# Sparse attention and a spectral mix on one core: channel weights read once, fewer constants, and a tail by pairs

## The chip, the cores and the metric

The kernel runs on one core of a Trainium2 chip. A core has TensorE (PE, matrix multiplication into PSUM), VectorE (DVE), ScalarE (ACT), GpSimd (POOL) and SyncE (SP), and 16 transfer engines (DMA) that move data between HBM and the on-chip memory. The metric is the device time of one execution in microseconds (us), the median of several runs.

## The reference, cut to what matters

Attention with two kinds of masks, then a spectral mixing layer over the result. B = 8, S = 576, 8 heads of 64, so D = 512, and 64 Fourier modes.

```python
# heads 0 to 3: local mask (0 <= i - j < 32); heads 4 to 7: strided (j <= i and i = j mod 32)
attn = softmax(where(mask, q @ k.T / 8, -1e9)); x = (attn @ v) as (8, 576, 512)

X = np.fft.rfft(x, axis=1)[:, :64]                    # real part Xr, imaginary part Xi
Yr = einsum('bmd,mde->bme', Xr, w_r) - einsum('bmd,mde->bme', Xi, w_i)
Yi = einsum('bmd,mde->bme', Xr, w_i) + einsum('bmd,mde->bme', Xi, w_r)
y = np.fft.irfft(Yr + 1j * Yi (zero above mode 63), n=576, axis=1)
u = x + y
out = u + np.maximum(u @ w_ch, 0.0)
```

w_r and w_i are 64 x 512 x 512 in fp32, 67 MB each: nearly all that the kernel reads. For mode 0 the imaginary part of X is zero, and the imaginary part of Y does not count.

## The kernel before

It works in fp16 on chip; transfers issued by GpSimd convert from fp32. There are three stages. First the strided heads of the 8 batches; the weights of the first 18 modes are fetched beside them. Then the local heads, with 8 modes per batch of the first half of the 512 input rows (slot 0) beside each. Then the same 64 modes over the other half (slot 1), with `turn` and `premix` beside them: x is transposed and multiplied with the channel weights ahead of time (v0 = x @ w_ch, xo = x). Last the tail, which adds the spectral part.

Constants and weight fetches:

```python
    # cM6: 128 x 432, cM5: 128 x 360 (a mask four times over), cMa: 128 x 480, cMb: 128 x 512, fp16
    ...
    pw = ctx.enter_context(tc.tile_pool(name="pw", bufs=NWBUF))        # 12 weight buffers of 512 KB
    ...
    GUEST = {3: ("Y0", 0), 4: ("Y0", 1), 5: ("X0", 0), 6: ("X0", 1)}   # weights that sit in
    GUEST |= {16: ("YT", 0), 17: ("YT", 1)}                            # space not yet used
    ...
            for ri, src in enumerate([moe_w_r, moe_w_i]):
                nc.gpsimd.dma_start(
                    wt[ds(64 * ri, 64)],
                    src[m, ds(256 * half, 256), :].rearrange("(p c) e -> p c e", c=4),
                )
    ...
    def w_cp_fetch():      # the channel weights, rows reordered to match the transposed x
        w_cp = pw.tile([128, 4, DM], F16, tag="w", name="w_cp")
        ...                # four transfers of 128 KB
```

One mode: 16 matmuls, then the fetch of a later weight tile; after eight modes the sum is taken out of PSUM.

```python
    def mode(slot, m):
        ...
        if slot or m not in GUEST:
            w_fetch()
        if mi == 7:
            ...
            if slot == 0:
                nc.scalar.activation(out=YS["Y0"][part], in_=src, func=ACTF.Copy)
            else:
                nc.vector.tensor_tensor(
                    out=YS["YT"][part], in0=src, in1=YS["Y0"][part], op=AluOp.add
                )
```

The local stage, 19 items of attention work per batch spread over 8 modes:

```python
        for mi in range(8):
            upto = -(-len(work) * (mi + 1) // 8)
            for w in work[n:upto]:
                w()
            n = upto
            mode(0, 8 * b + mi)
    ...
    w_chs["n"] = ptr.tile([128, 4, DM], F16, name="w_ch")       # the channel weights again,
    nc.gpsimd.dma_start(w_chs["n"], moe_w_ch.rearrange("(c p) e -> p c e", p=128))   # rows in order
```

The tail. A unit (b, t) is a tile of 128 rows of the output of batch b (t = 4: the last 64 rows of two batches). Spectra of the last 16 modes are first transposed (`tp`) and multiplied with the channel weights (`zp`), and copied per batch to yys and zzs.

```python
    psum_pools(z=2, v=3, u=3)
    ...
    def unit_v0(i):
        ...
        nc.tensor.matmul(vps[i], idn, v0, start=True, stop=(t == 4))     # L803

    def unit_v(i):
        ...
        rows_v(b, t, vp)                                                 # L634: += inverse DFT of zz
        ...
        nc.scalar.activation(out=rl, in_=vp, func=ACTF.Relu)             # L812
        if pool_adds(b, t):
            nc.gpsimd.tensor_tensor(out=rl, in0=rl, in1=xo, op=AluOp.add)    # L815

    def pool_adds(b, t):
        return t in (1, 3, 4) and (b, t) != (B - 1, 3)

    def unit_u(i):
        ...
        rows_u(b, t, up, add=not pool_adds(b, t))                        # identity of xo, then yy
        ...
        nc.vector.tensor_tensor(                                         # L827
            out=osb[:, t % 2, :], in0=up, in1=rls[b, t][:, t % 2, :], op=AluOp.add
        )
        ...                                                              # stores by SyncE

    for i in range(3):
        unit_v0(i)
    spec_last(0)
    spec_out(3, 0, *held[0])
    LAG = 2
    for i in range(len(units) + LAG):
        ...          # unit_v0(i), unit_v(i), the spectra of the next batch, unit_u(i - LAG)
```

Of the kernel before, what the change touches and what calls it, by code (L numbers as in the profile page):

```python
# [15 lines left out]
B = 8  # L16
# [13 lines left out]
def _host_consts():  # L30
    s = np.arange(S)
    m = np.arange(NM)
    ang = 2.0 * np.pi * np.outer(s, m) / S
    F3 = np.stack([np.sin(ang), np.cos(ang), -np.sin(ang)], axis=1)
    F3 = F3.reshape(S, 3 * NM)

    Fl = np.zeros((128, 5, 3 * NM))
    for t in range(5):
        Fl[: SCS[t], t] = F3[128 * t : 128 * t + SCS[t]]
    Fs = np.zeros((128, 6, 3 * NM))  # L40
    for rp in range(2):
        for j, (a, z) in enumerate(JG):
            r2 = np.arange(a, z)
            ss = (32 * np.arange(NCB)[None, :] + 2 * r2[:, None] + rp).reshape(-1)
            Fs[: len(ss), 3 * rp + j] = F3[ss]

    A = np.zeros((4, 2, 16, S))
    for mm in range(NM):  # L50
        e = np.zeros(S // 2 + 1, dtype=np.complex128)
        for ri, unit in enumerate((1.0, 1j)):
            e[mm] = unit
            A[mm // 16, ri, mm % 16] = np.fft.irfft(e, n=S)
    A = A.reshape(2 * NM, S)
    A[:, :512] = A[:, :512].reshape(128, 256, 2).transpose(0, 2, 1).reshape(128, 512)

    ms = []
    for nr in (6, 5):
        n = nr * NCB  # L60
        kc, kr = np.arange(n) // nr, np.arange(n) % nr
        qr, qc = np.arange(n) // NCB, np.arange(n) % NCB
        ok = (kr[:, None] == qr[None, :]) & (kc[:, None] <= qc[None, :])
        blk = np.zeros((128, n))
        blk[:n] = np.where(ok, 0.0, NEG)
        ms.append(np.tile(blk, (1, 4)))

    rel = np.arange(160)[None, :] - np.arange(128)[:, None]
    blk = np.where((rel >= 0) & (rel < STRIDE), 0.0, NEG)
    ma = np.tile(blk, (1, 3))  # L70
    last = np.full((128, 96), NEG)
    last[:64, 32:] = blk[:64, :64]
    mb = np.tile(np.concatenate([blk, last], axis=1), (1, 2))
    f16 = [a.astype(np.float16) for a in (Fl, Fs, A, ms[0], ms[1], ma, mb)]
    return f16 + [np.eye(128, dtype=np.float16)]
# [3 lines left out]
def kernel(  # L79
# [20 lines left out]
    def psum_pools(**bufs):  # L100
        pctx.close()
        pss.clear()
        for n, c in bufs.items():
# [9 lines left out]
    hosts = _host_consts()  # L113
    names = ["cFl", "cFs", "cA", "cM6", "cM5", "cMa", "cMb", "cI"]
    drams = {
# [10 lines left out]

    idn = cs["cI"]


# [34 lines left out]
    def w_fetch(n=1):  # L164
        for _ in range(n):
# [9 lines left out]
            else:  # L175
                wt = pw.tile([128, 4, DM], F16, tag="w", name="wt")
            for ri, src in enumerate([moe_w_r, moe_w_i]):
                nc.gpsimd.dma_start(  # L178
# [4 lines left out]

    def w_cp_fetch():
        w_cp = pw.tile([128, 4, DM], F16, tag="w", name="w_cp")
        for c2 in range(2):
            for half in range(2):
                nc.gpsimd.dma_start(
                    w_cp[ds(64 * c2, 64), ds(2 * half, 2), :],
                    moe_w_ch[ds(256 * half, 256), :].rearrange(  # L190
                        "(p cp c2) e -> c2 p cp e", cp=2, c2=2
                    )[c2],
                )
        w_chs["cp"] = w_cp

# [115 lines left out]
    def str_scores(b, t):  # L311
# [3 lines left out]
        n = (z - a) * NCB  # L315
        mask = cs["cM6"] if j == 0 else cs["cM5"]
        scp = psum("sc")
        nc.tensor.matmul(scp[:, 0 : 4 * n], idn, mask, start=True, stop=False)
        for h in range(4):
# [84 lines left out]
    def loc_scores(b, h, tail):  # L404
        par, hp = b % 2, h // 2
        scp = psum("sc")
        nc.tensor.matmul(  # L407
            scp if tail else scp[:, 0:480],
            idn,
            cs["cMb"] if tail else cs["cMa"],  # L410
            start=True,
# [90 lines left out]
    def mode(slot, m):  # L502
# [5 lines left out]
        yv = yp.rearrange("p (m e x) -> p m e x", m=8, e=4)  # L508
        wt = w_tiles[slot * NM + m]
        for e in range(4):  # L510
            for c in range(4):
                nc.tensor.matmul(  # L512
                    yv[:, mi, e, :],
                    wt[:, XC[c], ds(128 * e, 128)],
                    Xh[half][:, c, :, :, m],
                    start=(c == 0),
                    stop=(c == 3),
                )
        if slot or m not in GUEST:
            w_fetch()  # L520
        if mi == 7:
            part = (slice(None), slice(None), mg // 2, slice(None), ds(8 * (mg % 2), 8))
            src = yp.rearrange("p (m e x) -> p e x m", m=8, e=4)
            if slot == 0:
# [120 lines left out]

    def rows_u(b, t, up, add):
        cols = out_cols(t)
        if add:
            xo = xos[b][:, t, :] if t < 4 else xoh[b // 2]
            nc.tensor.matmul(up, idn, xo, start=True, stop=(t == 4))  # L650
        if t < 4:
            nc.tensor.matmul(up, cs["cA"][:, cols], yys[b], start=not add, stop=True)  # L652
            return
        for i in range(2):
# [3 lines left out]
                yys[b - 1 + i],  # L658
                start=not add,
                stop=True,  # L660
# [7 lines left out]
    load(1)  # L668
    const_load(nc.sync, "cMa", "cMb", "cFl", "cA")
    load(2)  # L670
# [57 lines left out]

    psum_pools(tp=2, sc=2, av=2, y=2)
    for b in range(B):  # L730
# [10 lines left out]
        if b == 6:  # L741
            work.insert(0, w_cp_fetch)
        n = 0
        for mi in range(8):
            upto = -(-len(work) * (mi + 1) // 8)
            for w in work[n:upto]:
                w()
            n = upto
            mode(0, 8 * b + mi)
    actx.close()  # L750
# [7 lines left out]
    yys = [ptr.tile([128, DM], F16, name=f"yy{i}") for i in range(B)]  # L758
    w_chs["n"] = ptr.tile([128, 4, DM], F16, name="w_ch")
    nc.gpsimd.dma_start(w_chs["n"], moe_w_ch.rearrange("(c p) e -> p c e", p=128))  # L760
    work = []
    for b in range(B):
# [11 lines left out]
    n = 0  # L774
    for m in range(NM):
        mode(1, m)
# [7 lines left out]

    psum_pools(z=2, v=3, u=3)
    units = []
    for b in range(B):
        units += [(b, 0), (b, 1)]
        if b % 2:
            units.append((b, 4))  # L790
        units += [(b, 2), (b, 3)]
    held, vps, rls, osbs = {}, {}, {}, {}
    LAST = len(units) - 1

    def spec_last(bq):
        held[bq] = psum("z", half=True), psum("z")
        spec_mm(3, bq, *held[bq])

    def unit_v0(i):
        b, t = units[i]  # L800
        vps[i] = psum("v")
        v0 = v0s[b][:, t, :] if t < 4 else v0h[b // 2]
        nc.tensor.matmul(vps[i], idn, v0, start=True, stop=(t == 4))  # L803

    def unit_v(i):
        b, t = units[i]
        vp = vps.pop(i)
        rows_v(b, t, vp)
        if t % 2 == 0:
            rls[b, t] = rls[b, t + 1] = pw.tile([128, 2, DM], FP, tag="w", name="rl")  # L810
        rl = rls[b, t][:, t % 2, :]
        nc.scalar.activation(out=rl, in_=vp, func=ACTF.Relu)  # L812
        if pool_adds(b, t):
            xo = xos[b][:, t, :] if t < 4 else xoh[b // 2]
            nc.gpsimd.tensor_tensor(out=rl, in0=rl, in1=xo, op=AluOp.add)  # L815

    def pool_adds(b, t):
        return t in (1, 3, 4) and (b, t) != (B - 1, 3)

    def unit_u(i):  # L820
        b, t = units[i]
        up = psum("u")
        rows_u(b, t, up, add=not pool_adds(b, t))
        if t % 2 == 0:
            osbs[b, t] = osbs[b, t + 1] = pw.tile([128, 2, DM], FP, tag="w", name="osb")
        osb = osbs[b, t]
        nc.vector.tensor_tensor(  # L827
            out=osb[:, t % 2, :], in0=up, in1=rls[b, t][:, t % 2, :], op=AluOp.add
        )
        if t == 4:  # L830
            for j in range(2):
                nc.sync.dma_start(
                    out[b - 1 + j, ds(512, 64), :], osb[ds(64 * j, 64), 0, :]
                )
        elif i >= LAST - 1:
            nc.sync.dma_start(
                out[b, ds(256, 256), :].rearrange("(p i) e -> p i e", i=2)[:, t % 2, :],
                osb[:, t % 2, :],
            )
        elif t % 2:  # L840
            nc.sync.dma_start(
                out[b, ds(128 * (t - 1), 256), :].rearrange("(p i) e -> p i e", i=2),
                osb,
            )

    for i in range(3):
        unit_v0(i)
    spec_last(0)
    spec_out(3, 0, *held[0])
    LAG = 2  # L850
    for i in range(len(units) + LAG):
        if i < len(units):
            b, t = units[i]
            if i > 2:
                unit_v0(i)
            unit_v(i)
            if t == 1 and b + 1 < B:
                if b + 1 == 4:
                    spec_last(1)
                spec_out(3, b + 1, *held[(b + 1) // 4])  # L860
        if i >= LAG:
            unit_u(i - LAG)

# [29 lines left out]
```

The softmax here doesn't subtract the row's maximum and nothing guards it: scores larger than these inputs give would overflow.

## Time and profile before

| | us |
|---|---|
| time, median of 3 runs | 451.14 (450.70 to 451.53) |
| span of the profiled execution | 448.4 |
| PE busy | 341.4 (76%) |
| DVE busy | 215.0 (48%) |
| ACT busy | 185.8 (41%) |
| POOL busy | 183.1 (41%) |
| transfer w_cp, 4 of 128 KB, issue to landing | 8.2 |
| transfer w_ch, 512 KB, issue to landing | 11.1 |

The profile is of one execution. Busy time is the sum of an engine's instructions; a transfer's own share is given for the 16 DMA engines together. A group of instructions is named by its line in the kernel, its engine and operation, what it writes and reads, and its count; behind the bar stand its busy time, the mean ns of one, and the idle time before it with what ended it. Line numbers (L827) are those of the kernel before.

### The profile page before, as it was taken

The numbers are of one execution on the slowest core, as the hardware profiler recorded it, in microseconds if no ns is written. First come the engines' busy times: TensorE is split into PE (matmuls) and PEld (weight loads), VectorE is DVE, ScalarE is ACT, GpSimd is POOL, SyncE is SP. The second block draws the span as 40 slices with busy tenths as digits, with TensorE's granted clock in tenths as the row PEclk, the third lists the DMA queues.
The fourth block names the chain that finished last, engine by engine and source line by source line (L and its number), as shares of the span: only waits on it lengthen the run. The fifth ranks groups of instructions, "written<-read, shape, count | busy, mean of one in ns | idle before, by whom it ended". The sixth has DMA issues, their size and how long they took to land.

```text
span 448.4 us, 12268 instructions
## 1 busy us (share of the span) xinstructions
PE 341.4 (76%) x5269; PEld 242.9 (54%) x5269; DVE 215.0 (48%) x461; ACT 185.8 (41%) x349; POOL 183.1 (41%) x332
## 2 busy tenths in 40 slices
PE   2887687769898986848875585877859687787994
PEld 2766576647676865646654353545536454543441
DVE  3687767846443542323311242336344543542895
ACT  1586666554554552514341120213314221342883
POOL 4233333332544343444444343434344444420773
PEclk9998979899987895756555575768797886888999
DMA  8999999999999999999999999999999999992687
GB/s 200 197 198 200 203 197 203 209 211 208 165 211 210 214 210 212 210 213 212 212 207 208 212 212 211 212 212 211 213 203 212 213 211 212 212 211 48 261 313 272
DMA packets 31637, 93.72 MB, mean 209 GB/s; under 512 B 5792, under 2 KB 7584, under 8 KB 31584
## 3 DMA queue, kind: packets, MB, share of 16 engines
q0 software_dynamic: 27344, 82.33, 94.1%
q1 hardware_dynamic: 3664, 10.09, 6.1%
q8 instruction: 41, 0.67, 0.6%
q10 hardware_dynamic: 576, 0.53, 0.4%
q14 instruction: 12, 0.10, 0.1%
HBM read 165.80 MB, written 9.44 MB: 391 GB/s over the span
## 4 chain that ended last, share of the span: by engine, by line
DMA 52%; PE 19%; issue 3%; ACT 2%; DVE 1%; POOL 0%; DVEq 0%; ACTq 0%; POOLq 0%
DMA wt<-in_moe_w_i_dram 43%; DMA wt<-in_moe_w_r_dram 6%; PE y L512 4%; DMA qn<-in_k_dram 2%; PE tp L362 2%; PE v L803 2%; PE sc L407 2%; PE v L634 1%; PE u L652 1%; PE y L480 1%; PE sc L423 1%; PE u L650 1%; PE av L444 1%; ACT X L233 1%; PE z L621 1%
## 5 line engine op out<-in xcount | busy, mean ns | idle before, releaser
L512 PE MATMUL y<-X,wt 128*128 128x16 f16 x2048 | 83.0, 192 | 67.2 <-DMA wt<-in_moe_w_i_dram 62.1
L178 POOL DMA_DIRECT2D wt<-in_moe_w_r_dram x128 | 66.3, 518 | 122.1 <-DMA wt<-in_moe_w_r_dram 30.4
L512 PEld LDWEIGHTS <-wt 128*128 128x128 f16 x2048 | 72.8, 103 | 79.7 <-issue 71.7
L178 POOL DMA_DIRECT2D wt<-in_moe_w_i_dram x128 | 66.2, 517 | 74.3 <-DMA wt<-in_moe_w_i_dram 41.3
L608 ACT ACTIVATE v<-sc 128x512 f16<-128x512 f32 x32 | 19.1, 597 | 88.2 <-PE sc L599 88.2
L599 PE MATMUL sc<-w_cp,xT 128*128 128x512 f16 (+1 forms) x160 | 52.4, 457 | 0.5 <-DVE xT L571 0.5
L437 ACT ACTIVATE PL<-sc 128x480 f16<-128x480 f32 (+1 forms) x48 | 27.3, 579 | 50.9 <-PE sc L423 49.7
L609 DVE COPY xo<-tp 128x512 f16<-128x512 f16 x32 | 22.1, 692 | 50.7 <-PE tp L607 50.7
L223 DVE TENSOR_TENSOR xb<-av,rec 90x256 f16<-90x256 f32 (+2 forms) x80 | 36.0, 450 | 2.8
L222 DVE RECIPROCAL rec<-av 90x4 f32<-90x4 f32 (+2 forms) x80 | 14.7, 184 | 42.0 <-PE av L452 29.0
L369 DVE COPY qT<-tp 128x576 f16<-128x576 f16 x16 | 12.1, 759 | 40.8 <-PE tp L362 36.7
L233 ACT ACTIVATE v<-tp 128x640 f16<-128x640 f16 (+1 forms) x24 | 19.4, 807 | 23.2 <-PE tp L396 19.7
L362 PE MATMUL tp<-cI_s,qn 64*64 64x64 f16 x864 | 25.9, 210 | 3.4 <-DMA qn<-in_q_dram 2.2
L327 ACT ACTIVATE PS<-sc 90x360 f16<-90x360 f32 (+1 forms) x48 | 22.7, 488 | 11.0 <-PE sc L320 10.5
L827 DVE TENSOR_TENSOR osb<-u,rl 128x512 f32<-128x512 f32 x36 | 23.3, 688 | 6.2 <-ACT rl L812 3.2
L815 POOL TENSOR_TENSOR rl<-rl,xo 128x512 f32<-128x512 f32 x15 | 17.3, 1158 | 20.0 <-ACT rl L812 19.6
L362 PEld LDWEIGHTS <-qn 64*64 64x64 f16 x864 | 20.3, 123 | 9.0 <-issue 3.8
L258 PE MATMUL tp<-cI_s,qn 72*128 72x72 f16 x256 | 15.1, 209 | 12.5 <-DMA qn<-in_v_dram 9.6
L627 ACT ACTIVATE zz<-av 32x512 f16<-32x512 f32 x24 | 14.1, 588 | 24.1 <-PE av L621 23.9
L369 DVE COPY vT<-tp 128x576 f16<-128x576 f16 x16 | 12.1, 758 | 23.5 <-PE tp L362 23.5
L423 PE MATMUL sc<-qT,kz 128*128 128x160 f16 (+1 forms) x160 | 23.0, 272 | 0.0
L599 PEld LDWEIGHTS <-xT 128*128 128x128 f16 (+1 forms) x160 | 14.7, 110 | 15.3 <-issue 7.2
(91 smaller groups left out, 659.3 us busy)
## 6 DMA issues: line engine op xcount, KB each, us to landing
wt<-in_moe_w_r_dram POOLq DMA_DIRECT2D x128, 256.0 KB, 9.4
wt<-in_moe_w_i_dram POOLq DMA_DIRECT2D x128, 256.0 KB, 9.6
out_dram<-osb SPq DMA_DIRECT2D x15, 512.0 KB, 2.7
qn<-in_v_dram POOLq DMA_DIRECT2D x16, 288.0 KB, 10.5
qn<-in_q_dram POOLq DMA_DIRECT2D x16, 288.0 KB, 10.8
qn<-in_k_dram POOLq DMA_DIRECT2D x16, 288.0 KB, 10.7
out_dram<-osb SPq DMA_DIRECT2D x8, 128.0 KB, 2.4
w_cp<-in_moe_w_ch_dram POOLq DMA_DIRECT2D x4, 128.0 KB, 8.2
```

What stands on the lines that cost most here:

```text
L178: nc.gpsimd.dma_start(wt[ds(64 * ri, 64)], src[m, ds(256 * half, 256), :].rearrange("(p c) e -> p c e", c=4),)
L223: nc.vector.tensor_tensor(out=dst, in0=val.rearrange("p h (q c) -> p h c q", c=4), in1=rec[0:n, 0:pieces] .to_broadcast((n, pieces, 64)) . ...
L233: nc.scalar.activation(out=out, in_=in_, func=ACTF.Copy)
L327: nc.scalar.activation(out=PS[0:n, ds(POFF[t], 4 * n)], in_=scp[0:n, 0 : 4 * n], func=ACTF.Exp, scale=SCALE,)
L362: nc.tensor.transpose(tp[ds(64 * hp, 64), ds(64 * i, 64)], qn[ds(64 * hp, 64), vi, ds(64 * (9 * g + i), 64)], idn[ds(64 * hp, 64), ds(64 * ...
L369: eng(out=dst.rearrange("p (h s i) -> p h s i", h=2, i=18)[:, :, :, ds(9 * g, 9)], in_=tp[pr, 0:576].rearrange("p (i h s) -> p h s i", h=2 ...
L423: nc.tensor.matmul(scp[:, ds(col, n)], kzs[par][:, hp, ds(s0, 128)], qTs[par][:, ds(s0, n)], start=False, stop=(i == len(todo) - 1),)
L437: nc.scalar.activation(out=dst, in_=src, func=ACTF.Exp, scale=SCALE)
L512: nc.tensor.matmul(yv[:, mi, e, :], wt[:, XC[c], ds(128 * e, 128)], Xh[half][:, c, :, :, m], start=(c == 0), stop=(c == 3),)
L599: nc.tensor.matmul(vp[pr, :], xT[:, ch, cols], w_chs["cp"][:, ch, :], start=(ch == 0), stop=(ch == 3),)
L609: nc.vector.tensor_copy(out=xo[pr].rearrange("p (h q c) -> p h q c", h=2, c=4), in_=tp[pr, 0:512].rearrange("p (h c q) -> p h q c", h=2, c=4),
L827: nc.vector.tensor_tensor(out=osb[:, t % 2, :], in0=up, in1=rls[b, t][:, t % 2, :], op=AluOp.add)
```

## The change

The channel weights are read from HBM once, in row order, and the reordered copy is made on chip by identity matmuls that pick rows. The imaginary weights of mode 0 are not read, and its matmuls take the 64 rows of the real part. The mask constants are kept for one head and read repeatedly by the mask matmul. The local stage gets 11, 9, 8, 8, 7, 7, 7, 7 modes beside its batches. The last mode is moved behind the tail's first identity passes, its sum is taken out in parts of 6 and 2 modes, and the channel product of the last spectra goes ahead of the transposes. The tail works by pairs of tiles: one ReLU for both, the u rows one step later. GpSimd adds x also for t = 2 of batches 1, 3 and 5. The two last stores go out from two queues. It is for fewer bytes and a shorter tail.

```diff
-        ms.append(np.tile(blk, (1, 4)))
+        ms.append(blk)
...
+    def mask_rows(name, n, times):
+        return cs[name][:, 0:n].unsqueeze(1).broadcast_to((128, times, n))
...
-            for ri, src in enumerate([moe_w_r, moe_w_i]):
+            for ri, src in enumerate([moe_w_r, moe_w_i] if m else [moe_w_r]):
...
-    def w_cp_fetch():
-        ...
+    def w_ch_fetch():
+        w_ch = pw.tile([128, 4, DM], F16, tag="w", name="w_ch")
+        nc.gpsimd.dma_start(w_ch, moe_w_ch.rearrange("(c p) e -> p c e", p=128))
+        w_chs["n"] = w_ch
...
+        ends = {7: 8}
+        if slot and mg == 7:
+            ends = {5: 6, 7: 2}
...
-    psum_pools(tp=2, sc=2, av=2, y=2)
+    psum_pools()
+    pss["y"] = ctx.enter_context(tc.tile_pool(name="ps_y", bufs=2, space=PSUM))
+    psum_pools(tp=2, sc=2, av=2)
+    NMODES = [11, 9, 8, 8, 7, 7, 7, 7]
...
-        for mi in range(8):
-            upto = -(-len(work) * (mi + 1) // 8)
+        for mi in range(nm):
+            upto = -(-len(work) * (mi + 1) // nm)
...
-    w_chs["n"] = ptr.tile([128, 4, DM], F16, name="w_ch")
-    nc.gpsimd.dma_start(w_chs["n"], moe_w_ch.rearrange("(c p) e -> p c e", p=128))
+    w_chs["cp"] = ptr.tile([128, 4, DM], F16, name="w_cp")
+    def w_turn(half, cp):
+        wp = psum("sc")
+        for c2 in range(2):
+            for i in range(2):
+                a = 64 * c2 + 32 * i
+                nc.tensor.matmul(
+                    wp[ds(a, 32), :],
+                    idn.rearrange("p (x c) -> p c x", c=4)[:, 2 * cp + c2, :],
+                    w_chs["n"][:, 2 * half + i, :],
+                    ...
+        act_copy(w_chs["cp"][:, 2 * half + cp, :], wp)
...
-    psum_pools(z=2, v=3, u=3)
+    psum_pools(v=2, u=2)        # v: tiles of two banks
+    steps = []
+    for b in range(B):
+        steps.append((b, (0, 1)))
+        if b % 2:
+            steps.append((b, (4,)))
+        steps.append((b, (2, 3)))
...
-        return t in (1, 3, 4) and (b, t) != (B - 1, 3)
+        if (b, t // 2) in ((0, 0), (B - 1, 1)):
+            return False
+        return t in (1, 3, 4) or (t == 2 and b in (1, 3, 5))
...
+        for i, k in ((0, 1), (1, 1)) if step == FIRST else ((0, n),):
+            nc.scalar.activation(
+                out=rl[:, ds(i, k), :], in_=vp[:, ds(i, k), :], func=ACTF.Relu
+            )
...
+    v_early(steps[0])
+    u_early(0, 0)
+    u_early(0, 1)
+    v_early(steps[1])
+    mode(1, NM - 1)
     spec_last(0)
     spec_out(3, 0, *held[0])
+    for i, step in enumerate(steps):
+        b, ts = step
+        if step not in vps:
+            v_early(step)
+        v_rows(step)
+        ...                      # the spectra of the next batch
+        if i > 0:
+            u_rows(steps[i - 1])
+    u_rows(LAST)
```

## The prediction

> **What bounds the kernel now.** I read the page first, then the windows, the chain, and last the timelines of GpSimd and of the tail. The page's second part gives the bandwidth in 40 slices of 11.2 us:
>
> ```profile
> DMA  8999999999999999999999999999999999992687
> GB/s 200 197 198 200 203 197 203 209 211 208 165 211 210 214 210 212 210 213 212 212 207 208 212 212 211 212 212 211 213 203 212 213 211 212 212 211 48 261 313 272
> ```
>
> The transfer engines are busy through the 36th slice and a little on, that is to about 408 us, at 200 to 213 GB/s (counted as fp16 written). One slice, the eleventh (112 to 123 us), falls to 165. The chain of waits says the same from 162 us on: 43% of the span is weight transfers by moe_w_i, 6% by moe_w_r. The last mode's matmuls start at 408.51 us, and the last modes come every 2.47 us, which is 0.524 MB (two transfers of 256 KB) at 212 GB/s. So up to 408.5 us a byte less is time less, at about 2.47 us per 0.524 MB.
>
> The windows of 4 us around the dip (columns: window, its length, busy us and count of PE, weight load, DVE, ACT, POOL, then clock, DMA share, GB/s):
>
> ```profile
> 108.00:112.00 4.00, 3.48 (x86) 2.81 (x83) 2.04 (x5) 1.74 (x3) 0.00 (x0) 1.00 1.06 210
> 112.00:116.00 4.00, 3.62 (x71) 2.66 (x69) 0.76 (x1) 3.27 (x8) 2.23 (x5) 1.00 0.71 121
> 116.00:120.00 4.00, 4.00 (x129) 3.58 (x127) 3.13 (x7) 1.86 (x4) 2.52 (x5) 1.00 1.00 183
> 120.00:124.00 4.00, 2.82 (x62) 1.98 (x60) 1.19 (x2) 1.54 (x4) 1.06 (x3) 0.82 1.09 198
> ```
>
> Against 212, the last three lack (91 + 29 + 14) x 4 us = 0.54 MB, 2.5 us. GpSimd's timeline shows why:
>
> ```profile
> 107.41 0.52 POOL L178 DMA_DIRECT2D wt<-in_moe_w_i_dram  x1 [0.65 <-DMA qn<-in_v_dram]
> 113.78 0.52 POOL L178 DMA_DIRECT2D wt<-in_moe_w_r_dram  x1 [5.85 <-PE y L512]
> ```
>
> It issues nothing for 5.85 us. In the code a weight fetch follows each mode except modes 3 to 6, whose weights sat in guest buffers, and mode 7 comes only after all of batch 0's local attention (at 112.83 us). A fetch lands some 10 us after its issue, so this hole outruns the queue.
>
> Then the tail, 40 us after the last weights. Its stretches, same columns:
>
> ```profile
> 408.50:413.00 4.50, 3.82 (x27) 1.69 (x28) 1.53 (x3) 0.58 (x1) 0.00 (x0) 0.62 0.00 0
> 413.00:442.60 29.60, 29.54 (x138) 11.88 (x137) 24.65 (x41) 24.27 (x43) 21.82 (x19) 1.00 0.73 277
> 442.60:448.40 5.80, 0.01 (x1) 0.00 (x0) 1.22 (x3) 0.00 (x0) 0.00 (x0) 0.86 0.65 221
> ```
>
> In the middle stretch TensorE never stops: 29.54 of 29.60 us at clock 1.00. That stretch is TensorE's; DVE (24.7), ACT (24.3) and GpSimd (21.8) follow behind it. Its groups:
>
> ```profile
> L827 DVE TENSOR_TENSOR osb<-u,rl 128x512 f32<-128x512 f32 x36 | 23.3, 688 | 6.2 <-ACT rl L812 3.2 <-POOL rl L815 1.9 <-PE u L652 0.8
> L812 ACT ACTIVATE rl<-v 128x512 f32<-128x512 f32 x36 | 20.2, 598 | 4.1 <-PE v L634 3.5 <-PE v L637 0.4
> L815 POOL TENSOR_TENSOR rl<-rl,xo 128x512 f32<-128x512 f32 x15 | 17.3, 1158 | 20.0 <-ACT rl L812 19.6
> ```
>
> **What the Trainium skill says.** "DMA: Bandwidth & Descriptors", Specifications, puts the fabric ceiling at 435 GB/s. The trace agrees if the fp32 side is counted: 212 GB/s written as fp16 is 424 GB/s read. So the stream has no slack, and only fewer bytes shorten it. "TensorE: Matmul & The Clock Gate", "Wait — 56ns, not 53.3ns?", gives 426.7 ns start to start at N = 512 cold and 215.7 warm. The trace agrees: 0.43 us each for the four matmuls after 410.4 us, 0.215 us in the tail's timeline. "PSUM — Partial Sum Buffer", Specifications: eight banks of 512 fp32. The tail before uses all eight (z 2, v 3, u 3); the tail after too (y 2, v 2 pairs, u 2), so u loses a bank. "Perfetto Trace Analysis", Optimization Strategy, warns that a gap repeated on the engine that should be saturated can mean too few PSUM buffers; no such gap is in this tail before, and I expect one after.
>
> **Part by part: the stream.**
> 1. Imaginary weights of mode 0, two transfers of 256 KB: 0.524 MB, -2.5 us.
> 2. The second reading of the channel weights, w_cp, 4 x 128 KB: 0.524 MB, -2.5 us. In its place come 16 identity matmuls and 4 ACT copies (about 0.6 us each, from the 128x512 copies of L608) in the second half of the modes, where TensorE is busy 182 of 248 us and ACT 69. They lie beside the stream: 0.
> 3. Masks: cM6 108 -> 27 KB, cM5 90 -> 22.5, cMa and cMb 248 -> cMl 64, 332 KB less. They are fp16 on both sides, and the first 12 us move up to 290 GB/s, so -1.2 us. The mask matmul streams as many columns as before.
> 4. Eleven modes instead of eight beside batch 0. By the order of work, mode 7 comes after 14 of 19 work items instead of 19. Those 14 items and five modes were done at 108.5 us; two more modes of 0.48 us put mode 7 at 109.5, 3.3 us earlier. The hole in the issues shrinks from 5.85 us to some 2.5 to 4, against a queue which items 1 and 3 leave about 2.5 us shorter. I take back most of the 2.5: -1.8 us.
>
> The share is 1.04 to 1.06 in every long window, so these add: -8.0 us, and the last weights come at about 400.5 us.
>
> **The tail.** Start: the last addition into YT shrinks from 128x512 (0.69 us) to 128x128 (I take 0.25), and the four channel matmuls go ahead of the four transposes, about 0.4 us. First zz-dependent matmul 3.65 us after the last mode's start instead of 4.49: -0.8 us.
>
> Middle, TensorE's work: 133 matmuls of 512 columns (36 identity passes of v0, 40 v rows and 40 u rows, since t = 4 takes two each, 17 identity passes of x) become 133 - 2 (21 GpSimd additions instead of 19) - 4 (v) - 2 (x), the last six all early, = 125, against 130 before after its 3 early ones; at 0.2155, -1.1 us if TensorE stays the bound. But does it? I walked one pair of batches by hand. The order per step is v early, v rows, then the u rows of the step before; u has two banks, so a unit's matmul waits for DVE's addition two units back. The hard step is (b,(2,3)) of b = 1, 3, 5, where both halves go through GpSimd. Let T be the end of its v rows on TensorE. ReLU of the pair starts T+0.2 and takes 1.02 (a 90x1024 ACT copy in the trace): 1.22. GpSimd: start 1.30, ends 2.46 and 3.60 (1.16 each, 1.14 when back to back). DVE: 2.50 to 3.19, and 3.65 to 4.34. TensorE, unhindered, would want those two banks at 2.58 (after u of t=4 0.43, v 0.86, u of this step 0.43, v 0.86) and 3.01; it gets them at about 3.26 and 4.41. Two waits of 0.7 us: 1.4 us. The next two single-GpSimd steps give another 0.07 and 0.19 (chain 0.2 + 1.02 + 0.08 + 1.16 + 0.05 + 0.69 + 0.07 = 3.27 against 3.2). Period of two batches 8.54 us, where the matmuls alone take 6.88. Three such periods: +5.0. The fill, walked the same way, loses 1.2 us until the first hard step (before: 0.2). Middle after: 26.9 + 1.3 (the second group of spectra) + 5.0 + 1.2, less 0.3 hidden behind those spectra, = 34.1 against 29.45: +4.6.
>
> End: the last two stores leave from two queues instead of one after the other (1.04 us for two issues now): -0.55.
>
> Tail: -0.8 + 4.6 - 0.55 = +3.2. Whole: 451.1 - 8.0 + 3.2 = 446.3.
>
> **Rivals.**
> - *The tail stays TensorE-bound.* Then it gains 0.8 + 1.1 + 0.55 = 2.4, and the whole is 440.7. For it: it is what the change was made for, and GpSimd's 21 x 1.16 = 24.4 us fit in 28. Against it: the chain of four engines behind two banks does not fit by the durations above. I give it 25%.
> - *The saved bytes leave the stream idle instead of shortening it*, because fetches wait for buffers. For it: the hole at 107.9 and another of 3.90 us before 328.67 us. Against it: only 2.5 and some 0.5 us were lost there, and everywhere else GpSimd waits for the queue. If items 3 and 4 brought nothing: 449.
> - *The clock.* A stuttering TensorE could fall to the half clock: the tail would run into 450. The waits are under 1 us each, so unlikely.
>
> **Range and chances.** The sum is 446.3. The first rival pulls the middle of my belief down to 445.6. Stream -8.0 +- 1.2 and tail +3.2 +- 1.5 on one side and the first rival on the other give 441.0 to 448.5. Two per cent faster is 442.1, which takes nearly the whole first rival: 0.24. Slower by 2%: 0.01.
>
> **What would show it.** The last mode's matmuls at 400 to 401 us instead of 408.5 (stream). No window under 190 GB/s between 100 and 130 us (item 4). The first zz-dependent matmul 3.6 to 3.7 us after the last mode. TensorE's busy share in the middle of the tail at 80 to 85% instead of 99.8%, its idle time released by DVE's addition and gathered behind the steps (b,(2,3)) of b = 1, 3, 5; the middle 33 to 35 us. I am wrong if TensorE is above 95% busy there, or if the last weights come later than 403 us.

## The result, and the profile after

| | before | after |
|---|---|---|
| time, median of 4 runs, us | 450.92 (450.59 to 451.53) | 448.15 (447.37 to 449.45) |
| span of the profiled execution, us | 448.4 | 446.2 |
| last mode's matmuls start | 408.51 | 403.14 |
| from there to the first matmul that needs the last spectra | 4.49 | 2.73 |
| middle of the tail (TensorE) | 29.45 | 35.03 |
| from there to the end | 5.95 | 5.30 |

The ratio is 0.994, with a 95% interval of 0.9914 to 0.9966: a gain of 0.6%. The last four rows add to the span on each side. The stream of weights got 5.4 us shorter, and the tail gave 3.17 of them back (-1.76 + 5.58 - 0.65). Line numbers from here on are those of the kernel after: L857 is the early identity pass of v, L648 and L651 are the v rows, L868 the ReLU, L873 GpSimd's addition, L880 the identity pass of x, L663 and L666 the u rows, L891 DVE's last addition, L847 the channel product, L180 the weight fetch.

The page's second part, in slices of 11.2 us:

```profile
DMA  8999999999999999999999999999999999992676
GB/s 182 180 203 200 200 199 207 211 210 204 171 213 211 212 212 211 212 210 212 213 210 212 212 212 211 212 212 213 212 207 212 212 212 212 212 180 77 263 255 260
```

Against before, two things stand out. The first two slices fell from 200 and 197 to 182 and 180: fewer bytes were moved there, and the time did not shrink with them. And the eleventh slice still dips, to 171 (before 165). The 4 us windows of the dip, with the columns that the prediction names:

```profile
104.00:108.00 4.00, 4.00 (x84) 3.12 (x83) 2.08 (x5) 1.95 (x3) 1.03 (x2) 0.50 1.08 214
108.00:112.00 4.00, 4.00 (x94) 3.52 (x92) 1.58 (x3) 1.25 (x3) 0.00 (x0) 0.50 0.95 188
112.00:116.00 4.00, 4.00 (x71) 3.55 (x68) 1.72 (x5) 2.01 (x3) 2.60 (x6) 0.52 0.75 135
116.00:120.00 4.00, 4.00 (x94) 3.12 (x94) 0.85 (x2) 2.99 (x7) 2.84 (x6) 1.00 1.03 187
```

GpSimd's timeline around it:

```profile
104.75 0.53 POOL L180 DMA_DIRECT2D wt<-in_moe_w_i_dram  x1
112.43 0.52 POOL L180 DMA_DIRECT2D wt<-in_moe_w_r_dram  x1 [7.16 <-PE y L515]
```

The hole in the fetches is 7.16 us, longer than the 5.85 of before, though mode 7 now has less work ahead of it. The clock column says why it could be: TensorE is granted 0.50 from 104 us on, where before it had 1.00 from 108, and the items ahead of mode 7 are TensorE's. From 100 to 108 us it ran 155 matmuls here; runs 1 and 3 below, with the same order of work at 0.88 and 0.91 of the clock, ran 202 and 229, and their holes were 4.18 and 2.66 us.

The tail's three stretches, same columns:

```profile
403.14:405.87 2.73, 1.90 (x24) 1.19 (x25) 0.70 (x2) 0.59 (x1) 0.00 (x0) 1.00 0.02 6
405.87:440.90 35.03, 30.44 (x133) 11.61 (x132) 25.68 (x43) 22.88 (x28) 23.81 (x21) 1.00 0.63 238
440.90:446.20 5.30, 0.17 (x1) 0.00 (x0) 0.87 (x2) 0.00 (x0) 0.00 (x0) 0.75 0.62 214
```

TensorE is busy 30.44 of 35.03 us in the middle, 87%, where it never stopped before. DVE (25.7), ACT (22.9) and GpSimd (23.8) are all well below the 35 us: no engine is full, so the stretch is bounded by waits. The groups of the tail:

```profile
L891 DVE TENSOR_TENSOR osb<-u,rl 128x512 f32<-128x512 f32 x36 | 23.6, 688 | 8.0 <-POOL rl L873 4.6 <-ACT rl L868 1.3 <-PE u L663 0.6
L873 POOL TENSOR_TENSOR rl<-rl,xo 128x512 f32<-128x512 f32 x17 | 19.3, 1158 | 21.1 <-ACT rl L868 21.1
L868 ACT ACTIVATE rl<-vp 128x1024 f32<-128x1024 f32 x15 | 15.3, 1025 | 9.9 <-PE vp L648 9.8
```

DVE's idle time, 8.0 us, is now released mostly by GpSimd (4.6). The ReLU of a pair takes 1.025 us, and GpSimd waits for it before it may start the first of its two additions. TensorE's own waits from 405 to 441 us (line and what it waited for: us in total, times, longest):

```profile
PE u L663 <- DVE osb L891: 2.1, 4, 0.6
PE u L880 <- DVE osb L891: 1.8, 4, 0.5
PE vp L648 <- ACT zz L641: 0.5, 1, 0.5
PE vp L857 <- ACT rl L868: 0.4, 1, 0.4
```

TensorE's timeline shows where the long ones are:

```profile
414.56 0.59 PE L648 MATMUL vp<-zz,cA_s 128*128 128x512 f16 x2
415.62 0.38 PE L880 MATMUL u<-xo,cI_s 128*128 128x512 f16 x1 [0.47 <-DVE osb L891]
415.84 0.38 PE L663 MATMUL u<-yy,cA_s 128*128 128x512 f16 x1
416.74 0.38 PE L663 MATMUL u<-yy,cA_s 128*128 128x512 f16 x1 [0.52 <-DVE osb L891]
...
425.30 0.38 PE L880 MATMUL u<-xo,cI_s 128*128 128x512 f16 x1 [0.53 <-DVE osb L891]
...
426.41 0.38 PE L663 MATMUL u<-yy,cA_s 128*128 128x512 f16 x1 [0.52 <-DVE osb L891]
...
433.84 0.38 PE L880 MATMUL u<-xo,cI_s 128*128 128x512 f16 x1 [0.48 <-DVE osb L891]
...
434.95 0.38 PE L663 MATMUL u<-yy,cA_s 128*128 128x512 f16 x1 [0.52 <-DVE osb L891]
```

Three pairs of waits, each behind a step (b,(2,3)) of b = 1, 3, 5, whose two tiles both go through GpSimd. The other two waits on DVE, 0.56 us at 411.31 and 0.30 us at 440.47, lie ahead of the first pair and in the last step. TensorE issues one such matmul every 0.2155 us, while a lone one is shown with 0.38 us to its end. So the wait shown as 0.52 us costs more of issue time: 416.74 - 415.84 - 0.2155 = 0.68 us.

### The profile page after: what moved, and what is told of

It is laid out like the page before. It is cut to its first block, busy times and chain, and to the rows that moved or that the text cites. A ratio compares the mean times of both kernels' runs of the same rounds, so it can differ in the third digit from the quotient of the medians.

```text
span 446.2 us, 12273 instructions
## 1 busy us (share of the span) xinstructions
PE 343.9 (77%) x5283; PEld 245.1 (55%) x5283; DVE 215.2 (48%) x462; ACT 187.1 (42%) x338; POOL 182.2 (41%) x328
## 4 chain that ended last, share of the span: by engine, by line
DMA 69%; PE 15%; issue 8%; POOL 3%; DVE 2%; ACT 2%; POOLq 0%; DVEq 0%; ACTq 0%
DMA wt<-in_moe_w_i_dram 44%; DMA wt<-in_moe_w_r_dram 9%; DMA qn<-in_q_dram 8%; DMA qn<-in_k_dram 5%; PE y L515 3%; PE tp L363 3%; POOL rl L873 3%; DMA qn<-in_v_dram 2%; PE sc L409 1%; PE sc L482 1%; PE sc L425 1%; DVE osb L891 1%; PE y L482 1%; POOL qn L200 1%; PE av L446 1%
## 5 line engine op out<-in xcount | busy, mean ns | idle before, releaser
L515 PE MATMUL y<-X,wt 128*128 128x16 f16 (+1 forms) x2048 | 82.9, 192 | 60.2 <-DMA wt<-in_moe_w_i_dram 57.2
L180 POOL DMA_DIRECT2D wt<-in_moe_w_r_dram x128 | 66.4, 519 | 132.3 <-PE y L515 26.8
L515 PEld LDWEIGHTS <-wt 128*128 128x128 f16 (+1 forms) x2048 | 72.9, 103 | 73.1 <-issue 50.3
L180 POOL DMA_DIRECT2D wt<-in_moe_w_i_dram x126 | 65.4, 519 | 63.2 <-DMA wt<-in_moe_w_i_dram 38.6
L613 PE MATMUL sc<-w_cp,xT 128*128 128x512 f16 (+1 forms) x160 | 53.5, 464 | 0.7 <-DVE xT L585 0.7
L873 POOL TENSOR_TENSOR rl<-rl,xo 128x512 f32<-128x512 f32 x17 | 19.3, 1158 | 21.1 <-ACT rl L868 21.1
L891 DVE TENSOR_TENSOR osb<-u,rl 128x512 f32<-128x512 f32 x36 | 23.6, 688 | 8.0 <-POOL rl L873 4.6
L328 ACT ACTIVATE PS<-sc 90x360 f16<-90x360 f32 (+1 forms) x48 | 22.9, 490 | 10.1 <-PE sc L321 9.5
L482 PEld LDWEIGHTS <-xb 108*128 108x128 f16 (+2 forms) x176 | 18.2, 120 | 12.3 <-DVE xb L218 6.3
L868 ACT ACTIVATE rl<-vp 128x1024 f32<-128x1024 f32 (+1 forms) x21 | 18.8, 903 | 11.5 <-PE vp L648 10.5
```

The costliest lines, as they stand in the source:

```text
L180: nc.gpsimd.dma_start(wt[ds(64 * ri, 64)], src[m, ds(256 * half, 256), :].rearrange("(p c) e -> p c e", c=4),)
L328: nc.scalar.activation(out=PS[0:n, ds(POFF[t], 4 * n)], in_=scp[0:n, 0 : 4 * n], func=ACTF.Exp, scale=SCALE,)
L482: nc.tensor.matmul(xp[:, ds(192 * cp, 192)], xb[b][0:n, base + t, ds(128 * cp, 128)], F[0:n, t, :], start=(i == 0), stop=(i == len(tiles) ...
L515: nc.tensor.matmul(yv[:, mi, e, :], wt[pr, XC[c], ds(128 * e, 128)], Xh[half][pr, c, :, :, m], start=(c == 0), stop=(c == 3),)
L613: nc.tensor.matmul(vp[pr, :], xT[:, ch, cols], w_chs["cp"][:, ch, :], start=(ch == 0), stop=(ch == 3),)
L873: nc.gpsimd.tensor_tensor(out=rl[:, i, :], in0=rl[:, i, :], in1=x_rows(b, t), op=AluOp.add)
```

## The experiments

Each experiment changes the kernel after, unless said. A is the theory of the prediction, that two u banks behind the chain TensorE, ACT, GpSimd, DVE bound the middle of the tail. Of the rivals, B puts the loss on something other than GpSimd's additions, C takes GpSimd's rate and not the banks for the limit, and D and E concern the stream and the early passes (runs 6 and 11). "Last mode" is the start of its matmuls in the experiment's profile; after has 403.14. Kernels of one batch were run on one chip beside the kernel before; on the chip of runs 9 to 12, before itself measured 451.51 (448.59 to 454.19), so ratios to before are compared rather than times.

### The tail

**1. GpSimd adds x for t = 1, 3, 4 only**: no step has both halves on GpSimd.

```diff
-        return t in (1, 3, 4) or (t == 2 and b in (1, 3, 5))
+        return t in (1, 3, 4)
```

> The changed kernel, with GpSimd adding x for t = 1, 3 and 4 only; TensorE adds it for t = 2 again. Theory A (a step whose both halves go through GpSimd holds the two u banks too long, 1.4 us in each of three steps): those waits go, three identity passes of 0.215 us come, so the middle of the tail is 35.0 - 4.2 + 0.65 = 31.5 us and the time 448.15 - 3.5 = 444.6 us. Rival B (the waits come from working by pairs with a lag of one step, whichever engine adds x): the waits stay, 448 to 449 us.

Measured 446.11, ratio 0.9891 (0.9872 to 0.9911). Middle and end of its tail:

```profile
405.27:437.40 32.13, 30.43 (x136) 11.92 (x135) 25.61 (x43) 22.85 (x28) 20.69 (x18) 1.00 0.68 259
437.40:443.80 6.40, 0.14 (x1) 0.00 (x0) 0.85 (x2) 0.00 (x0) 0.00 (x0) 0.69 0.52 182
```

Three more matmuls, and the middle is 2.9 us shorter (35.03 to 32.13): giving GpSimd three additions fewer and TensorE three passes more is a gain. The six long waits are gone; what is left on DVE is three of 0.56, 0.23 and 0.31 us. Only some 2 us of time came of it, for the end grew from 5.3 to 6.4. A had named 31.5 for the middle and 444.6 for the time: the direction is A's, the size a little less.

**2. The stream of after with the tail of before**: units of one tile, three v and three u banks, last mode ahead of the tail.

```diff
-    psum_pools(v=2, u=2)
+    psum_pools(z=2, v=3, u=3)
...
-        for i, k in ((0, 1), (1, 1)) if step == FIRST else ((0, n),):
-            nc.scalar.activation(
-                out=rl[:, ds(i, k), :], in_=vp[:, ds(i, k), :], func=ACTF.Relu
-            )
+        nc.scalar.activation(out=rl, in_=vp, func=ACTF.Relu)
...
+        return t in (1, 3, 4) and (b, t) != (B - 1, 3)
```

> The changed kernel's stream with the tail of the kernel before (single units, u 3 banks, no early passes, last mode in the loop). Theory: the tail alone lost 43.06 - 39.9 = 3.15 us, so 448.15 - 3.15 = 445.0 us, and the last mode starts at about 403 us as in the changed kernel. Rival (part of the loss is the last mode's later start, which the tail's early passes delay): then more comes back, 443 to 444 us.

Measured 445.11, ratio 0.9872 (0.9853 to 0.9891), with the last mode at 403.21.

```profile
403.21:407.57 4.36, 3.48 (x27) 1.57 (x28) 1.53 (x3) 0.59 (x1) 0.00 (x0) 0.69 0.02 4
407.57:437.20 29.63, 29.63 (x138) 11.95 (x137) 24.44 (x40) 24.23 (x43) 21.80 (x19) 0.99 0.72 274
```

The old tail brings the old full TensorE back, 29.63 of 29.63 us, on a stream that ends when after's does. So the new tail by itself costs about 3 us (ratio 0.994 against 0.9872), and the stream by itself gains 5.8.

**3. One ReLU per tile instead of one per pair**, banks and additions as in after. This lets GpSimd start about 0.4 us earlier (a ReLU of one tile takes 0.597 us, of a pair 1.025).

```diff
-        for i, k in ((0, 1), (1, 1)) if step == FIRST else ((0, n),):
+        for i, k in [(i, 1) for i in range(n)]:
```

> The changed kernel, with a ReLU for each half of a pair, still two u banks. By the walk with single ReLUs (0.60 us each, 0.52 apart) GpSimd starts 0.6 us sooner; of the two waits of 0.7 us in each hard step one goes: 0.78 in place of 1.4, and the small waits of 0.26 per pair of batches go too. Theory A (chain of ReLU, GpSimd and DVE behind two banks): 448.15 - 3 x 0.88 = 445.5 us. Rival C (the pair ReLU is harmless, GpSimd's own rate is what is too slow): within 0.7 us of 448.15.

Measured 447.08, ratio 0.9909 (0.9884 to 0.9933); the middle 33.77, that is -1.3 where A had -2.6. TensorE's timeline of this kernel has one wait per hard step instead of two:

```profile
401.56 1.04 PE L857 MATMUL vp<-v,cI_s 128*128 128x512 f16 x2 [0.25 <-DVE xoh L623]
...
417.33 0.38 PE L663 MATMUL u<-yy,cA_s 128*128 128x512 f16 x1 [0.52 <-DVE osb L891]
...
426.53 0.38 PE L663 MATMUL u<-yy,cA_s 128*128 128x512 f16 x1 [0.53 <-DVE osb L891]
...
434.63 0.38 PE L663 MATMUL u<-yy,cA_s 128*128 128x512 f16 x1 [0.52 <-DVE osb L891]
```

The first of the two waits goes when the chain starts earlier; the second, which hangs on GpSimd's two additions one after the other, stays. In time the run lies between A and C and does not separate them. The first line shows one reason: in this execution the early passes ran at half clock (1.04 us for two; 0.61 in after), and the last mode behind them began only at 404.10.

**4. Three u banks and v tiles of one bank**, with the same 21 additions on GpSimd. The six banks are split three and three instead of four and two.

```diff
-    psum_pools(v=2, u=2)
+    psum_pools(v=3, u=3)
...
-        vp = pss["v"].tile([128, 2, DM], FP, tag="v", name="vp")
+            vp.append(psum("v"))
...
+        for i in range(n):
+            nc.scalar.activation(out=rl[:, i, :], in_=vp[i], func=ACTF.Relu)
```

> As the run with a ReLU for each half, and with v tiles of one bank (3 of them) so that u has 3 banks; GpSimd's 21 additions stay, the early passes are 3 of v and 2 of x. Theory A (two banks): TensorE is the bound again, middle of the tail 28.4 + some 0.5 us for the fill, so 448.15 - 6.1 = 442.0 us and TensorE busy above 96% there. Rival C (GpSimd's rate, 4.64 us of additions in an odd batch against 3.9 us of matmuls): most waits stay, 445 us or more.

Measured 445.35, ratio 0.9874 (0.9853 to 0.9895). By its time it sits at C's number, so the profile has to decide. TensorE's waits from 405 to 437 us, all of them:

```profile
PE v L648 <- ACT zz L641: 0.4, 1, 0.4
PE v L857 <- ACT rl L868: 0.3, 1, 0.3
```

And its windows:

```profile
405.19:436.00 30.81, 30.44 (x134) 11.73 (x133) 24.99 (x43) 23.86 (x43) 23.95 (x21) 0.95 0.68 264
436.00:442.80 6.80, 0.12 (x1) 0.00 (x0) 1.17 (x2) 0.00 (x0) 0.00 (x0) 0.73 0.61 200
```

No wait on DVE is left, and TensorE is busy 30.44 of 30.81 us, with GpSimd as loaded as in after (23.95 against 23.81). So GpSimd's rate was not the bound. This run also has the single ReLUs of run 3, which alone took one of the two waits in each hard step; the third bank took the other. What kept it from A's 442: the first 3 us of it ran at half clock (mean 0.95 over the 30.81 us, about 1.5 us lost), and the end is 6.80 instead of 5.30. It comes out equal to the old tail of run 2 (445.11): with enough banks the new tail breaks even, and does not gain.

**11. The last mode ahead of the six early passes**, where after has it behind them.

```diff
+    mode(1, NM - 1)
     v_early(steps[0])
     ...
-    mode(1, NM - 1)
```

> The changed kernel with the last mode ahead of the early identity passes, all else kept. Theory E: TensorE is at half clock at the last mode, the channel product takes 1.7 us instead of 0.9 and waits behind six passes of 0.43 us: first v row 4.0 to 4.8 us after the last mode instead of 2.73, 449.5 us. Rival (it is only the place of the passes, hidden behind the last sum): 448.15 within 0.5 us.

Measured 450.61, ratio 0.9981 (0.9964 to 0.9997). TensorE's timeline of this kernel:

```profile
402.66 0.64 PE L515 MATMUL y<-X,wt 128*128 128x16 f16 x16 [1.46 <-DMA wt<-in_moe_w_i_dram]
403.14 1.01 PE L857 MATMUL vp<-v,cI_s 128*128 128x512 f16 x2
...
405.65 1.91 PE L847 MATMUL y<-w_ch,YT 128*128 128x512 f16 x4
...
408.24 1.02 PE L648 MATMUL vp<-zz,cA_s 128*128 128x512 f16 x4 [0.25 <-ACT zz L641]
```

The same place in after:

```profile
403.14 0.64 PE L515 MATMUL y<-X,wt 128*128 128x16 f16 x16
404.16 1.04 PE L847 MATMUL y<-w_ch,YT 128*128 128x512 f16 x4 [0.39 <-DVE YT L543]
...
405.87 1.02 PE L648 MATMUL vp<-zz,cA_s 128*128 128x512 f16 x4 [0.45 <-ACT zz L641]
```

From the last mode to the first v row it takes 5.58 us instead of 2.73, more than E's 4.0 to 4.8. The passes stand in the way for 2.5 us (403.14 to 405.65), for TensorE runs at half clock there (1.01 us for two of them, 0.61 in after); and the four channel matmuls take 1.91 instead of 1.04. The clock around it, columns as above:

```profile
398.00:402.00 4.00, 3.21 (x36) 1.88 (x32) 1.25 (x2) 0.59 (x1) 0.00 (x0) 0.50 0.31 60
402.00:408.00 6.00, 5.33 (x30) 2.41 (x31) 0.29 (x1) 0.40 (x1) 0.00 (x0) 0.50 0.01 3
```

The half clock is there from 398 us on, before TensorE waits its 1.46 us, so in this execution the wait did not cause it. Yet the order and the clock go together in the profiles: the four channel matmuls took 1.04 us in all ten kernels that have passes ahead of the last mode, and 1.91 in all four that have them behind it (before, and runs 2, 8 and 11). That the passes keep the clock up is argued from this; how, no run shows. The two profiles differ by 2.85 us at this spot; the ratios differ by 0.0041, about 1.9 us, with intervals that just touch.

### The stream

**5. The masks as before, four times over**, in the kernel after.

```diff
-        ms.append(blk)
+        ms.append(np.tile(blk, (1, 4)))
...
-        mask = mask_rows("cM6" if j == 0 else "cM5", n, 4)
+        mask = cs["cM6"] if j == 0 else cs["cM5"]
```

> The changed kernel with the masks stored in full again (340 KB more of constants), all else kept. By the prediction (they cost 1.2 us of the stream): 449.3 us. By the cumulated bytes of the two profiles (at 16 us the kernel before had moved 3.18 MB, the changed one 2.85, so the stream behind the constants was no further): at most 0.4 us slower than 448.15.

Measured 448.6, ratio 0.9949 (0.9919 to 0.9978), which is after's ratio within both intervals; last mode 402.44, if anything earlier. In its first 16 us 3.17 MB were moved, in after's 2.85, in before's 3.18. The ratio alone could hide the 1.2 us; but the extra bytes were moved within the same 16 us, and the last mode was no later. The 0.32 MB cost nothing that can be measured: they do not lie where bytes set the pace. What does set it in those 16 us was not looked for.

**6. Guest buffers for modes 2, 4, 6, 8 instead of 3 to 6**, so that no four modes in a row are without a fetch. D is the theory that the dip at 108 us comes from that gap in the fetches.

```diff
-    GUEST = {3: ("Y0", 0), 4: ("Y0", 1), 5: ("X0", 0), 6: ("X0", 1)}
+    GUEST = {2: ("Y0", 0), 4: ("Y0", 1), 6: ("X0", 0), 8: ("X0", 1)}
```

> The changed kernel with the four weight tiles that sit in guest buffers given to modes 2, 4, 6 and 8 instead of 3, 4, 5 and 6, so that no two modes without a fetch follow each other. Theory D (the dip at 108 to 120 us comes from four modes in a row without a fetch, and its depth from the clock TensorE happens to have there: 7.2 us of hole at half clock, under 3 at full): the hole is under 4 us at any clock, no window of 4 us under 200 GB/s between 100 and 130 us, last mode at 402.4 instead of 403.1, time 447.4 us. Rival (the hole comes from elsewhere): the windows dip as before, 448.15 us.

Measured 448.55, ratio 0.9939 (0.9909 to 0.997): no change in time, though an interval this wide could hide D's 0.75 us. Its windows:

```profile
104.00:108.00 4.00, 4.00 (x84) 3.31 (x84) 1.24 (x4) 2.59 (x4) 1.26 (x4) 0.50 1.09 216
108.00:112.00 4.00, 4.00 (x93) 3.90 (x92) 1.90 (x4) 1.89 (x3) 1.40 (x3) 0.50 1.07 211
112.00:116.00 4.00, 4.00 (x76) 3.12 (x74) 0.84 (x3) 2.23 (x6) 1.74 (x4) 0.90 1.05 202
116.00:120.00 4.00, 4.00 (x111) 3.40 (x109) 2.79 (x6) 1.65 (x5) 1.95 (x4) 1.00 1.06 205
```

TensorE is at half clock through 112 us as in after, and yet the dip is filled: from 96 to 128 us 6.69 MB against 6.21, and no hole in GpSimd's fetches over 2.6 us. D's mechanism holds. But the last mode comes at 402.07, only 1.1 us earlier, and the median shows none of it. It moves less later: 40.53 MB from 128 to 320 us against 40.67 (the transfers of the two traces, summed), and 0.1 less from 320 to 336 us. About half of the 0.5 MB is lost again.

**10. Eight modes beside each batch**, as before.

```diff
-    NMODES = [11, 9, 8, 8, 7, 7, 7, 7]
+    NMODES = [8] * 8
```

> The changed kernel with 8 modes beside every batch. If 11 modes beside batch 0 brought nothing, as the dip in the profile of the changed kernel says: 448.15 within 0.7 us, a hole of 6 to 8 us. By the prediction (1.8 us): 449.9 us.

Measured 449.57, ratio 0.9962 (0.994 to 0.9985); last mode 402.69, a hole of 6.11 us at full clock, 6.43 MB from 96 to 128 us. The ratio is 0.0022 above after's, about 1 us, with overlapping intervals. Whether the new split brings about 1 us or nothing stays open; the 1.8 us of the prediction are at the edge of it.

**7. The imaginary weights of mode 0 read again** (and not used), two transfers of 256 KB.

```diff
-            for ri, src in enumerate([moe_w_r, moe_w_i] if m else [moe_w_r]):
+            for ri, src in enumerate([moe_w_r, moe_w_i]):
```

> The changed kernel, reading the imaginary weights of mode 0 again (0.524 MB more) and not using them. Theory (the stream is bound by its bytes): +2.5 us, 450.6 us, last mode at 405.6. Rival (the two transfers fall into slack, as the masks did): 448 to 449 us.

Measured 450.54, ratio 0.9985 (0.996 to 1.001); last mode 405.53, that is +2.4. The theory named both, and the rival falls.

**12. The channel weights read twice again**, w_cp by four transfers, without the matmuls that reorder them.

```diff
-    def w_ch_fetch():
-        w_ch = pw.tile([128, 4, DM], F16, tag="w", name="w_ch")
+    def w_cp_fetch():
+        w_cp = pw.tile([128, 4, DM], F16, tag="w", name="w_cp")
...
-    w_chs["cp"] = ptr.tile([128, 4, DM], F16, name="w_cp")
+    w_chs["n"] = ptr.tile([128, 4, DM], F16, name="w_ch")
+    nc.gpsimd.dma_start(w_chs["n"], moe_w_ch.rearrange("(c p) e -> p c e", p=128))
```

> The changed kernel, reading the channel weights twice as before and without the turn on chip. By their bytes (0.524 MB at 212 GB/s): +2.4 us, 450.6 us. Rival (the turn on chip costs something in the stream): less than 1.5 us slower.

Measured 451.05, ratio 0.9982 (0.9967 to 0.9997); last mode 406.24, +3.1. Runs 7 and 12 together: 0.52 MB in the stream costs 2.4 to 3.1 us of it, and 0.0042 to 0.0045 of the ratio, 1.9 to 2.0 us. In run 12 the 16 reordering matmuls and four copies are gone as well, and it is no better off than run 7: they cost nothing that shows.

### A version from the parts

**8. The stream of after, guests apart as in run 6, the tail of run 2** with after's channel product ahead of the transposes, its last sum in parts of 6 and 2, and its last stores on two queues.

```diff
-    GUEST = {3: ("Y0", 0), 4: ("Y0", 1), 5: ("X0", 0), 6: ("X0", 1)}
+    GUEST = {2: ("Y0", 0), 4: ("Y0", 1), 6: ("X0", 0), 8: ("X0", 1)}
...
-    psum_pools(v=2, u=2)
+    psum_pools(z=2, v=3, u=3)
```

> A version meant to beat both: the changed kernel's stream with guests apart, the tail before by single units with three u banks, and of the new tail only the parts that cost no bank: the last sum in parts of 6 and 2 modes, the channel product ahead of the transposes, the last two stores from two queues. From the run with the tail before, 445.1: -0.7 (guests) -0.4 -0.4 -0.5 = 443.1 us. If the reordering is hidden by other waits: 444.5.

Measured 444.46, ratio 0.9856 (0.9829 to 0.9882). Start 3.93, middle 29.66, end 5.80 us, against 4.36, 29.63 and 6.20 in run 2: the reordering and the smaller last sum go with 0.43 at the start, the second queue with 0.40 at the end, in these profiles. The time is at the 444.5 of the rival; the 443.1 that was hoped for did not come.

**9. The same with three early passes of v ahead of the last mode**, as after has six.

```diff
+    psum_pools(v=3, u=3)
...
+    mode(1, NM - 1)
     spec_last(0)
```

> The version with reordered units, and three identity passes of v0 ahead of the last mode (y keeps its two banks, the spectra use them, v 3, u 3). Theory E (what the early passes bring is a TensorE at full clock when the last weights land: 2.73 us from the last mode to the first v row against 3.93 with the passes after it): 444.5 - 1.2 = 443.3 us. Rival (the passes themselves delay the last mode when TensorE is cold): 444 to 446 us.

Measured 444.15 (443.62 to 444.53), ratio 0.9827 (0.9792 to 0.9862), the lowest of all kernels here.

```profile
402.15:404.88 2.73, 1.90 (x24) 1.19 (x25) 0.70 (x2) 0.58 (x1) 0.00 (x0) 0.96 0.02 6
404.88:435.70 30.82, 30.82 (x138) 12.25 (x137) 25.01 (x42) 24.67 (x43) 21.94 (x19) 0.95 0.69 264
435.70:441.80 6.10, 0.15 (x1) 0.00 (x0) 1.36 (x3) 0.00 (x0) 0.00 (x0) 0.76 0.65 222
404.68:408.10 3.42, 3.22 (x8) 1.13 (x8) 1.32 (x3) 2.46 (x6) 1.15 (x1) 0.50 0.00 0
```

The start is after's 2.73 and TensorE is never idle in the middle. But the middle is 30.82 instead of 29.66, since its first 3.2 us ran at half clock (fourth line, with the last 0.2 us of the start). Run 8 had its half clock in the start (0.61 in the mean of the 3.93 us). So what the start gained here the middle lost: from the last mode to the end it takes 39.65 us, in run 8 39.39. That early passes bring E's 1.2 us of time is not shown by this run. Its gain over the kernel before is 1.7%, and its interval ends below after's begins; against run 8, and by a little against run 2, the intervals overlap.

## Why the prediction was right, and where its steps were not

The time, 448.15, lies in the range of 441.0 to 448.5, near its upper end and 2.55 us above the 445.6. The plain sum of the steps, 446.3, was closer. That it lies inside is partly luck. The stream brought 2.6 us less than its steps said; the start brought about 1 us more and the middle cost about 1 us more, which cancel. The two profiled spans differ by 2.2 us, the medians by 2.8; with 2.2, the 451.1 that the prediction starts from would have come to 448.9, outside the range. The pull from there toward the first rival went the wrong way: the tail did not stay TensorE-bound (87% busy, waits released by DVE's addition), and runs 1 and 4 show why. Of the signs named, the waits came where they were expected, and the middle (35.03) and the busy share (87%) lie just beyond the 33 to 35 us and the 80 to 85%; the last mode at 400 to 401 us, no window under 190 GB/s (135 was seen), and 3.6 to 3.7 us at the start failed.

**The stream: -5.4 instead of -8.0.** "Imaginary weights" and "the second reading" (steps 1 and 2, -2.5 us each) hold; putting them back moved the last mode by 2.4 and 3.1 us. (That 424 GB/s leave no slack under the cited ceiling of 435 depended on which side of a transfer is counted, since 212 GB/s are written on chip. Runs 7 and 12 show by time that there was none. And the "200 to 213 GB/s" of the slices is 197 to 214 in the lines shown.) "Masks" (step 3, -1.2 us) failed: I read the 290 GB/s of the first 12 us, a peak of slices under 1 us (229 to 247 in the windows of 4 us from 4 to 12 us), as a rate that bytes have to pay for, but there they are not what is waited for; run 5 gives 0. "Eleven modes instead of eight" (step 4, -1.8 us) failed in the profile: the hole became 7.16 us, not 2.5 to 4, and the work ahead of mode 7 ran at half clock, a term that I had not put in. With the same split the hole was 2.66 to 4.18 us in runs 1, 3, 4 and 7 (0.88 to 0.93 of the clock from 100 to 108 us), about as predicted, and 4.20 to 5.86 in runs 2, 11 and 12 (0.50 to 0.52); run 5 does not fit, with 5.71 at 0.90. But a shorter hole brought little: in runs 1 and 4 the last mode came 0.6 and 0.7 us earlier than in after, and run 6, with the dip filled, gave no time. Run 10 leaves the step 0 to 1 us. These two steps are 3.0 us of the sum; 2.6 is what is missing. The last mode at 403.14 is just past the 403 that I had named for being wrong, and by that sign the stream's part was wrong.

**The start: -1.76 instead of -0.8.** The two steps that I named, the smaller sum and the channel product ahead of the transposes, are alone in run 8 and give 0.56 (4.49 to 3.93). The rest comes with the passes ahead of the last mode, which I had counted as work and not as a gain at the start: I let the channel product run at half clock, as in the tail before (0.43 us each), and behind the passes it took 1.04 us instead of 1.91. Runs 11 and 9 show the term at the start by taking it away (5.58) and by giving it to the old tail (3.93 to 2.73); in run 9 the half clock then fell into the middle.

**The middle: +5.6 instead of +4.6.** The walk's mechanism and its sizes are there: the ReLU of a pair 1.025 us (predicted 1.02); the two waiting matmuls at T + 3.23 and T + 4.35 behind the first hard step, whose v rows end at T = 412.39 (predicted 3.26 and 4.41); the period of two batches 8.54 us from 425.30 to 433.84 (predicted 8.54). The 0.93 us that the middle of 34.1 was short come from its edges: until the first hard step 6.52 us for 23 matmuls of 0.2155, a loss of 1.56 instead of 1.2; 0.1 in the periods; and 0.5 after the last v rows at 439.13, where six matmuls take 1.77 us to 440.90 instead of 1.29: one more wait on DVE, of 0.30 us as shown. Run 4 shows the cause by removing it: with a third u bank and single ReLUs the waits on DVE are gone at the same load of GpSimd. "Perfetto Trace Analysis", Optimization Strategy, in the Trainium skill, which the prediction named for gaps that repeat where buffers are too few, fits this tail.

**The end: -0.65, predicted -0.55.** But it isn't a cost of its own: kernels whose middle is shorter end with a longer last stretch (6.1 to 6.8 in runs 1, 2, 4 and 9), perhaps as their stores have had less time to drain. I argue this from the windows; no run tests it. The one pair with equal middles, run 8 against run 2, gives the second queue 0.40.

**The rivals.** The TensorE-bound tail fell. "The saved bytes leave the stream idle" was right for steps 3 and 4, as it said (449, with the tail as predicted). "The clock" was asked of the tail's middle, where it stayed at 1.00 in after; in runs 4 and 9 it fell to 0.50 for some 3 us there, with no wait of TensorE over 0.45 us behind the last mode. In after it stood at 0.50 at the stream's dip, and at 1.00 in the start, which was cheaper for it.

## What to carry to other kernels

Before freeing an engine by moving an addition to a slower one, walk one period of the chain with its measured durations and count the buffers that it holds meanwhile: GpSimd had room for 21 additions, but two banks behind ReLU, GpSimd and DVE did not, and the tail lost 3 us while every engine had idle time. Where TensorE waits for a last transfer, try matmuls that need nothing in that wait, ahead of the awaited work and not behind it: here about 1.9 us by the ratios of run 11 and after. But look at the clock of the whole tail: in run 9 the gain at the start was lost again in the middle, and in run 3 passes at half clock held up the last mode, by about 1 us (an estimate: 404.10 against the 402.44 to 403.21 of runs 1, 2, 4 and 5). In a stream bound by transfers, count only the bytes that lie in its steady part: 0.52 MB there were 2 to 3 us, 0.32 MB at the start were nothing that could be measured.

## What the runs showed of the hardware that was not expected

The size of the dip at 108 us changes from kernel to kernel with the same instructions in that stretch. With TensorE at 0.50 to 0.52 from 100 to 108 us the runs moved 6.21 (after), 6.40 (2 and 12) and 6.56 MB (11) between 96 and 128 us; with 0.88 to 0.93 they moved 6.66 (1), 6.72 (7) and 6.75 (3 and 4). Run 5 is an exception, with 6.43 at 0.90. So the clock that TensorE happens to be granted may reach the transfers, through the fetches that are issued behind its work; the figures are of one execution each, and the link is argued from them.

GpSimd's fetches pause near 176 and near 329 us in every profile, before's too (4.55 and 3.88 us in after; 3.17 to 4.55 and 3.86 to 4.03 over all). In after the trace shows nothing that released them; in some of the other runs it names a transpose of TensorE. What GpSimd waits for there was not found.

Filling the dip gave back about half of its bytes later in the stream, and no time that the medians show. What takes the rest is open too.
